# Moving one step of the weight preparation from the first pass of attention tiles to the second

## The chip, the core and the metric

One core of a Trainium2 chip runs the whole program. The metric is the device time of one execution, in microseconds (us). Engines are named as the profile names them: PE multiplies matrices, PEld loads its weights, DVE is the vector engine, ACT the scalar engine, POOL the GpSimd engine, SP the engine from whose queue (SPq) most DMAs are issued. "L390" is line 390 of the kernel's file.

## The reference

Attention with a threshold over 8 batches and 8 heads (576 positions, 64 elements a head), then a SwiGLU feed-forward block over the 4608 tokens of 512 elements that it gives.

```python
# q, k, v: (8, 8, 576, 64) float32
scores = scale * np.matmul(q, k.transpose(0, 1, 3, 2))          # scale = 1/8
thresh = np.max(scores, axis=-1, keepdims=True) - tau           # tau = 0.02
scores = np.where(scores >= thresh, scores, -1000000000.0)
scores = scores - np.max(scores, axis=-1, keepdims=True)
attn = np.exp(scores)
attn = attn / (np.sum(attn, axis=-1, keepdims=True) + 1e-09)
x = np.matmul(attn, v)            # -> (8*576, 512): heads side by side
g = x @ w_gate                    # (512, 1536)
silu = g * (1.0 / (1.0 + np.exp(-g)))
val = x @ w_val                   # (512, 1536)
out = (silu * val) @ w_out        # (1536, 512)
```

The three weight matrices arrive as 64-bit floats. The kernel reads them as pairs of 32-bit words and makes 32-bit floats of them on the chip.

## The kernel before

**The tiles.** The queries of one head pair are worked off in tiles of 128 rows, the last one of 64. For a tile of both heads PE makes scores in PSUM (L505; L513 for the tile of 64), DVE takes the negated row maxima (L497), ACT makes the threshold (L528) and the exponentials (L529), and DVE's mask (L532) zeroes what is under the threshold and sums the rows; L534 and L535 give the reciprocal of the sum. The tile is then scaled (in the second pass the first head on ACT at L542, the second on POOL at L540), turned by PE (L576, L578 and the matmuls after them), copied by ACT (L585, L592) and multiplied with v (L609, L611). Gate and value matmuls of the feed-forward block (L625) fill PE between the tiles of the second pass.

**The stages.** Batch 0 has its order written by hand (up to L895); from L896 on a planner with job costs orders the rest. Batch 0 runs in eight segments, `segs`: n = 0 to 3 are the first pass, with the first two tiles (x = 0, 1) of each of the four head pairs; n = 4 to 7 are the second pass, with the remaining three tiles (x = 0, 1, 2; the last has 64 rows). "(4,1)" below is tile x = 1 of segment n = 4. In the loop at L815 to L889 a tile goes through four points: "maxima" (after the maxima were issued), "flipped" (after the exponentials, and the turning of the tile before), "masked" (after the masks) and "end". At each point `steps(n, x, point)` (L799) issues what the table `STEPS` (L128) has for it. Each engine and each DMA queue works in the order in which instructions were issued to it, and waits for semaphores where it needs another's result.

**The weights.** `wpieces` (L311) cuts the weights into 24 pieces. The first 16 are for gate and value, each with 128 x 384 64-bit numbers of both matrices (768 KB); below they are numbered p0, p1, ... in the order in which they are fetched. A piece goes through five stages, each with its queue:

- fetch (`fetch_weights`, L332): two DMAs of 384 KB on SP (L344), into one of four landing places in turn, and only if the place is free; "weights 2" asks for two pieces.
- split (`split_weights`, L355): ACT takes the high words (L360). The low words go through POOL (L362) in the first pass, and through ACT (L364) in the second. In the first pass POOL's clamp (L353) follows at once; in the second the piece is put on the list `unclamped`, and the clamp is issued when `clamp_split` (L370) is next called: after the masks of a tile (L870), or by a shift that needs it.
- shift (`shift_weights`, L376): DVE, L383, after the clamp.
- join (`join_weights`, L386): DVE, L390, with the sign; it frees the landing place for the next fetch.
- sum (`add_lower`, L397): POOL, L400, adds the low words; the piece can then be used.

In the first pass only the table issues these stages. In the second the loop does it for each tile: a join after the maxima (L830), a split and up to two fetches before "flipped" (L860), and after the masks (L866 to L873) a join where a piece is shifted, fetches, the clamps outstanding, a sum, and a shift. Other entries of the table: "rest", "v" and "qk" start loads on SP (L436, L479, L480), "scale" is a scaling of loaded q on POOL (L440), "prepare" and "turn" are transposes on DVE (L738, L742, L797). PE starts a tile's scores into the PSUM that the masks of an earlier tile read, so it can wait for L532.

Of the kernel before, what the change touches and what calls it, by code (L numbers as in the profile page):

```python
# [27 lines left out]
class Plan:  # L28
# [101 lines left out]
    (0, 1, "maxima"): ("prepare",),  # L130
    (0, 1, "masked"): ("split",),
    (0, 1, "end"): ("scale",),
    (1, 0, "flipped"): ("split", "shift"),
    (1, 0, "masked"): ("join",),
    (1, 1, "flipped"): ("weights 2", "prepare"),
    (1, 1, "masked"): ("split", "shift"),
    (1, 1, "end"): ("join",),
    (2, 0, "maxima"): ("rest", "weights 2"),
    (2, 0, "flipped"): ("rest",),
    (2, 0, "masked"): ("shift", "scale", "split", "join"),  # L140
    (2, 0, "end"): ("weights 2",),
    (2, 1, "maxima"): ("scale", "prepare", "v", "rest"),
    (2, 1, "flipped"): ("rest", "split"),
    (3, 0, "flipped"): ("shift",),
    (3, 0, "end"): ("join",),
    (3, 1, "maxima"): ("shift", "split", "turn last"),
    (3, 1, "flipped"): ("weights 2", "scale", "prepare"),
    (3, 1, "masked"): ("split",),
    (3, 1, "end"): ("turn", "shift", "scale"),
    (4, 0, "flipped"): ("turn", "qk"),  # L150
    (4, 1, "maxima"): ("scale",),
    (4, 1, "masked"): ("scale",),
    (4, 2, "end"): ("turn",),
# [2617 lines left out]
```

## Time and profile before

| | |
|---|---|
| time, median of 3 runs | 1332.68 us (1331.83 to 1333.17) |
| the profiled execution, its own time | 1332.23 us |
| span of its trace | 1330.4 us |
| granted PE clock | 1.00 |
| first pass of batch 0 (scores of (0,0) to those of (4,0)) | 7.0 to 46.3 us |
| second pass of batch 0 (until the first L2111) | 46.3 to 123.5 us |
| fetches of pieces from SP (L344) | 16 times two, issue to landing 3.2 / 4.2 / 6.6 us (min, median, max) |

The scores (L505, L513) start at these times in the trace: (0,0) 7.00, (1,0) 15.24, (2,0) 25.48, (2,1) 30.74, (3,0) 36.04, (3,1) 41.52, (4,0) 46.29, (4,1) 56.44, (4,2) 61.03, (5,0) 66.73, (5,1) 73.87. A PE that starts a score group and finds a wait inside shows a longer group, not idle time. Times in timelines are microseconds from the start of the span; in brackets stand the idle time ahead of an instruction and what ended it. Busy times of PE come from a model of its pipeline, so that a busy PE need not be at its peak.

### The profile page before, as it was taken

Reading aid. Unit: us, or ns where it says so; the run is one execution under the profiler, and the core shown is the slowest. Engines: PE = TensorE matmul, PEld = TensorE weight load, DVE = VectorE, ACT = ScalarE, POOL = GpSimd, SP = SyncE. Lnnn points to the kernel's source line nnn. Section 1 sums busy time; section 2 is a strip of 40 time slices with the busy share of each in tenths; the row PEclk is TensorE's granted clock in tenths of the full one; section 3 lists DMA queues with packets and bytes.
Section 4 is the critical chain, followed back from the end, with each engine's and each line's share of the span. In section 5 each row is a group of like instructions: output and inputs, shape, how many; then the busy total and the mean of one; then the engine's idle time right before and its main releaser. Section 6 shows DMA issues by size and latency. Waiting matters only on the chain.

```text
span 1330.4 us, 41756 instructions
## 1 busy us (share of the span) xinstructions
PE 1320.2 (99%) x16294; PEld 1119.1 (84%) x16294; DVE 1092.4 (82%) x2900; ACT 892.9 (67%) x2336; POOL 951.1 (71%) x1137
## 2 busy tenths in 40 slices
PE   8999999999999999999999999999999999999998
PEld 7777777777788878888888888887888889999998
DVE  7799988878887788878888887888788888767986
ACT  6898877677755777787777777777777775444300
POOL 3788597565695979756995779677975798866720
PEclk9999999999999999999999999999999999999999
DMA  8853334456647544656265746655465627465341
GB/s 178 220 180 108 71 81 120 126 155 178 161 168 228 168 152 114 202 157 222 71 203 165 235 107 193 180 166 154 111 202 157 217 74 227 152 208 189 96 171 40
DMA packets 230884, 209.81 MB, mean 158 GB/s; under 512 B 167968, under 2 KB 185376, under 8 KB 223008
## 3 DMA queue, kind: packets, MB, share of 16 engines
q1 hardware_dynamic: 226768, 206.22, 52.4%
q8 instruction: 129, 2.11, 0.7%
q10 hardware_dynamic: 3920, 0.92, 0.3%
q14 instruction: 67, 0.55, 0.1%
HBM read 169.08 MB, written 38.01 MB: 156 GB/s over the span
## 4 chain that ended last, share of the span: by engine, by line
PE 94%; ACT 3%; DMA 1%; POOL 1%; DVE 1%; SPq 1%; issue 0%; ACTq 0%; DVEq 0%
PE pb L1190 14%; PE px L1820 12%; PE sc L2111 10%; PE pa L1190 10%; PE xa L2211 10%; PE pe L1190 6%; PE po L1498 6%; PE sc L2601 5%; PE py L1820 4%; PE pe L1385 3%; PE pb L2601 2%; PE pg L1423 2%; PE pa L2601 2%; PE pv L1423 2%; PE py L1829 2%; PE sc L1820 1%
## 5 line engine op out<-in xcount | busy, mean ns | idle before, releaser
L2159 DVE SCALAR_TENSOR_TENSOR pall<-sc,th,pall 128x288 f32<-128x288 f32 x504 | 244.2, 514 | 39.3 <-ACT pall L2157 20.2
L2157 ACT ACTIVATE pall<-sc,nm 128x288 f32<-128x288 f32 x504 | 232.7, 497 | 34.9 <-DVE pall L2159 34.7
L1190 PE MATMUL pb<-xall,big 128*128 128x256 f32 x864 | 205.9, 381 | 0.0
L2189 DVE STREAM_TRANSPOSE pall<-pall 128x576 f32<-128x576 f32 x252 | 188.4, 764 | 19.2 <-ACT pall L2187 9.4
L971 POOL TENSOR_TENSOR big<-big 128x128 f32<-128x128 f32 (+3 forms) x226 | 167.1, 748 | 43.5 <-ACT big L1325 21.7
L2187 ACT ACTIVATE pall<-pall,ri 128x288 f32<-128x288 f32 x380 | 175.8, 527 | 27.3 <-DVE ri L2175 26.3
L1190 PEld LDWEIGHTS pb<-xall,big 128*128 128x128 f32 x864 | 161.0, 190 | 24.1 <-issue 2.2
L971 POOL TENSOR_TENSOR hall<-hall,tmp 128x512 f32<-128x512 f32 x80 | 102.1, 1278 | 87.9 <-DVE hall L1249 66.9
L2132 DVE TENSOR_REDUCE mx<-sc 128x2 f32<-128x576 f32 x168 | 125.5, 747 | 45.2 <-PE sc L2111 45.1
L2111 PE MATMUL sc<-kT,qT 64*32 64x288 f32 (+1 forms) x5376 | 144.5, 345 | 0.0
L1190 PE MATMUL pa<-xall,big 128*128 128x256 f32 x576 | 137.6, 382 | 0.0
L2111 PEld LDWEIGHTS sc<-kT,qT 64*32 64x32 f32 x5376 | 95.3, 106 | 48.3 <-issue 8.3
L2211 PE MATMUL xa<-pall,vall 64*32 64x288 f32 x4032 | 128.7, 404 | 0.0
L1190 PEld LDWEIGHTS pa<-xall,big 128*128 128x128 f32 x576 | 107.9, 190 | 17.3 <-issue 2.2
L2211 PEld LDWEIGHTS xa<-pall,vall 64*32 64x32 f32 x4032 | 74.0, 107 | 46.9 <-issue 4.0
L2184 POOL TENSOR_SCALAR pall<-pall,ri 128x288 f32<-128x288 f32 x124 | 63.5, 523 | 49.0 <-DVE ri L2175 46.9
L2168 ACT COPY sums<-sums 32x6 f32<-32x6 f32 x336 | 66.6, 198 | 31.3 <-DVE pall L2159 26.2
L1190 PE MATMUL pe<-xall,big 128*128 128x256 f32 x352 | 83.9, 381 | 0.0
L2134 DVE TENSOR_REDUCE mx<-sc 128x1 f32<-128x288 f32 x168 | 75.0, 447 | 0.0
L1190 PEld LDWEIGHTS pe<-xall,big 128*128 128x128 f32 x352 | 66.3, 190 | 10.3 <-ACT xlast L2223 0.7
L971 POOL TENSOR_TENSOR hall<-hall 128x384 f32<-128x384 f32 (+2 forms) x69 | 70.3, 1032 | 0.8
L971 POOL TENSOR_TENSOR big<-hall 128x384 f32<-128x384 f32 (+2 forms) x69 | 65.6, 972 | 4.3 <-PE pa L1190 4.2
(402 smaller groups left out, 3055.7 us busy)
## 6 DMA issues: line engine op xcount, KB each, us to landing
big<-sums_hbm SPq DMA_DIRECT2D x30, 1280.0 KB, 7.6
big<-sums_hbm SPq DMA_DIRECT2D x30, 1024.0 KB, 7.4
vall<-in_v_dram SPq DMA_DIRECT2D x112, 144.0 KB, 4.0
big<-sums_hbm SPq DMA_DIRECT2D x54, 256.0 KB, 3.6
sums_hbm<-big SPq DMA_DIRECT2D x36, 256.0 KB, 3.6
out_dram<-big SPq DMA_DIRECT2D x32, 256.0 KB, 3.1
qT<-in_q_dram SPq DMA_DIRECT2D x112, 72.0 KB, 4.2
kT<-in_k_dram SPq DMA_DIRECT2D x112, 72.0 KB, 3.0
```

Source lines behind the costliest of these rows:

```text
L971: nc.gpsimd.tensor_tensor(out=out, in0=a, in1=b, op=op)
L1190: nc.tensor.matmul(ps[:, i], w[:, k_, i * P:(i + 1) * P], x[:, k_, :], start=first and i == k_ == 0, stop=True, skip_group_check=True)
L1498: nc.tensor.matmul(ps, h(f), w[:, f, :], start=(f == 0), stop=(f == NF2 - 1))
L1820: nc.tensor.matmul(ps, a[:, f, :], ws[n][:, f, :], start=bank_ not in begun, stop=True, skip_group_check=True)
L2111: nc.tensor.matmul(pss[h][(slice(g * G, (g + 1) * G), *part)], qT[hs, col:col + G], kT[hs, c * SH + keys[0]:c * SH + keys[1]], start=True, ...
L2132: rs.append(job("DVE", 0.72, lambda n=n, tile_=tile_: nc.vector.tensor_reduce(out=mx[:, n:n + 2, 0], in_=tile_[:, :, 0:SH], axis=AX.X, op= ...
L2157: ej = job("ACT", 0.42, lambda x=x, n=n: nc.scalar.activation(ps[x], scs[x], AF.Exp, bias=nm[:, n:n + 1]), ej, masks.get((h, u - 1)), rank=0)
L2159: masks[x] = job("DVE", 0.45, lambda x=x, n=n: nc.vector.scalar_tensor_tensor(out=ps[x], in0=scs[x], scalar=th[:, n:n + 1], in1=ps[x], op0 ...
L2187: scaled.append(job("ACT", 0.46, lambda x=x, n=n: nc.scalar.activation(x, x, AF.Copy, scale=ri[:, n:n + 1]), rj, rank=rank))
L2189: seg["turned"].append(job("DVE", 0.72, lambda both=both: nc.vector.transpose(out=both, in_=both), *scaled, rank=rank))
L2211: nc.tensor.matmul(holds[a].ap()[x * G:(x + 1) * G, 0:SH].rearrange("d (i q) -> d i q", q=G), vr[rs, h, j, ds], p[rs, h, :, j, :], start=( ...
L2601: nc.tensor.matmul(both.ap(b_)[:, at_ * P:(at_ + 1) * P], ws[x], xd[x], start=b_ not in begun, stop=True, skip_group_check=True)
```

## The change

Four entries of the table differ in what they hold; in the others only a comma is added. At (2,0) "masked", a shift, a split and a join are taken out, and the scaling stays. The request for two pieces at (2,0) "end" is taken out. At (4,0) "end" there is a new entry: a join, a request for two pieces, a shift and a split. Since the stages take pieces in order, every later stage of the first pass works on the piece before the one that it worked on. From the middle of (4,0) the new steps bring the pieces back to where they were: with them p5 is joined, p6 shifted and p7 split, and from (4,2) on both kernels hold the same pieces in the same stages.

```diff
     (2, 0, "flipped"): ("rest",),
-    (2, 0, "masked"): ("shift", "scale", "split", "join"),
-    (2, 0, "end"): ("weights 2",),
+    (2, 0, "masked"): ("scale",),
...
     (4, 0, "flipped"): ("turn", "qk",),
+    (4, 0, "end"): ("join", "weights 2", "shift", "split",),
     (4, 1, "maxima"): ("scale",),
```

PE's instructions and their order are the same in both. One split moves from the first pass, where its low words are POOL's (L362), to the second, where they are ACT's (L364). A landing place becomes free only with a join, so that of the fetches one, of two DMAs, is really moved: from SP's queue ahead of the v loads of (2,1) to behind the loads of q and k that "qk" starts at (4,0).

More of the change, by code (lines that the diff above doesn't have):

```diff
@@ L132 @@
     (0, 1, "end"): ("scale",),
-    (1, 0, "flipped"): ("split", "shift"),
+    (1, 0, "flipped"): ("split", "shift",),
     (1, 0, "masked"): ("join",),
-    (1, 1, "flipped"): ("weights 2", "prepare"),
-    (1, 1, "masked"): ("split", "shift"),
+    (1, 1, "flipped"): ("weights 2", "prepare",),
+    (1, 1, "masked"): ("split", "shift",),
     (1, 1, "end"): ("join",),
-    (2, 0, "maxima"): ("rest", "weights 2"),
+    (2, 0, "maxima"): ("rest", "weights 2",),
     (2, 0, "flipped"): ("rest",),
-    (2, 0, "masked"): ("shift", "scale", "split", "join"),
-    (2, 0, "end"): ("weights 2",),
-    (2, 1, "maxima"): ("scale", "prepare", "v", "rest"),
-    (2, 1, "flipped"): ("rest", "split"),
+    (2, 0, "masked"): ("scale",),
+    (2, 1, "maxima"): ("scale", "prepare", "v", "rest",),
+    (2, 1, "flipped"): ("rest", "split",),
     (3, 0, "flipped"): ("shift",),
     (3, 0, "end"): ("join",),
-    (3, 1, "maxima"): ("shift", "split", "turn last"),
-    (3, 1, "flipped"): ("weights 2", "scale", "prepare"),
+    (3, 1, "maxima"): ("shift", "split", "turn last",),
+    (3, 1, "flipped"): ("weights 2", "scale", "prepare",),
     (3, 1, "masked"): ("split",),
-    (3, 1, "end"): ("turn", "shift", "scale"),
-    (4, 0, "flipped"): ("turn", "qk"),
+    (3, 1, "end"): ("turn", "shift", "scale",),
+    (4, 0, "flipped"): ("turn", "qk",),
+    (4, 0, "end"): ("join", "weights 2", "shift", "split",),
     (4, 1, "maxima"): ("scale",),
```

## Prediction, made before the changed kernel was run

> **What bounds the kernel now.** I read the busy shares and the chain of waits on the page first, then the windows of the first 140 us (the change touches nothing later), then the timelines of DVE, POOL and ACT around the two places that the diff names.
>
> ```profile
> PE 1320.2 (99%) x16294; PEld 1119.1 (84%) x16294; DVE 1092.4 (82%) x2900; ACT 892.9 (67%) x2336; POOL 951.1 (71%) x1137
> PE 94%; ACT 3%; DMA 1%; POOL 1%; DVE 1%; SPq 1%; issue 0%; ACTq 0%; DVEq 0%
> ```
>
> PE is busy for 99% of the span and holds 94% of the chain that ends last. So a microsecond is lost only where PE is made to idle, or to hold a matmul open on a wait, and such a loss is not won back: nothing behind it has slack on PE. The windows (start:end, length, then busy time and instructions of PE, PEld, DVE, ACT, POOL, the granted clock, DMA share, GB/s) show who is next to PE in each stage:
>
> ```profile
> 30.00:40.00 10.00, 9.91 (x87) 7.84 (x87) 9.57 (x24) 9.13 (x24) 5.35 (x7) 1.00 0.87 206
> 50.00:60.00 10.00, 9.63 (x71) 7.76 (x70) 6.29 (x14) 6.68 (x15) 6.66 (x5) 1.00 0.93 213
> 60.00:70.00 10.00, 10.00 (x85) 7.46 (x85) 7.34 (x18) 10.00 (x20) 7.80 (x6) 1.00 0.73 235
> ```
>
> Where work leaves, 30 to 40, DVE is nearly full (9.57 of 10). Where it arrives, 50 to 60, every engine but PE has over 3 us free. Right behind that, 60 to 70, ACT has nothing free at all.
>
> **Part 1, what is removed behind the masks of tile (2,0).** DVE loses one shift and one join ahead of the maxima of (2,1). Columns: start, duration, engine, line, operation.
>
> ```profile
> 31.31 0.54 DVE L383 TENSOR_SCALAR big<-big 128x768 uint32<-128x768 uint32 x1
> 31.89 0.96 DVE L390 SCALAR_TENSOR_TENSOR big<-wo,big 128x768 uint32<-128x768 uint32 x1
> 32.76 1.41 DVE L497 TENSOR_REDUCE nm<-sc 128x1 f32<-128x576 f32 x2
> ```
>
> The first maximum needs the first head's scores, whose last matmul ends at 31.98 (start 31.574 plus 0.403), so it could start at about 32.02 and not at 32.76: 0.74 earlier. Behind it come the turnings at L738 and L742 and the masks of (2,1), which end at 36.62 (35.81 + 0.81). PE waits for that end: the score group of (3,0) starts at 36.04 and takes 1.94, while the same eight matmuls of (3,1) take 1.25. PE itself is free at 35.88, its second head starts at 36.78. With the masks 0.7 earlier, some 0.7 of this stall goes (at most 0.85: from a free PE at 35.88 an unstalled group ends at 37.13 and not at 37.98; at the least 0, if the exps on ACT, 0.71 idle before their threshold for DVE, slip behind something else). I take -0.7. Until (4,1) the windows show PE full, so it is carried along. ACT loses a 0.97 split from the first pass and POOL a 0.9 low-word step, a clamp and a sum of 1.83; PE waits for none of them there, so they count nothing. On SP only one fetch of two loads leaves its place (38.56 and 38.96, 0.8 together) ahead of the v loads of L479; the places of the ring hold the others back.
>
> **Part 2, what is added at the end of (4,0).** ACT splits one more piece: L360 0.82 plus L364 0.91 to the next start, 1.73, in the 1.89 that it idles before L585 at 58.48. That idle hides it; without it 1.7 would show. The moved fetch is issued behind eight loads of q and k that SP issues until 58.1 (it then takes the place of the one at 58.27), so each fetch of the second pass brings the piece before the one it brought; see the third rival. DVE gets the join of p5 (0.96; pieces are numbered from 0 as they are fetched) and the shift of p6 (0.55), 1.5 in its 3.64 idle before 57.71, by busy time hidden twice over. But the shift waits for POOL's clamp (L353) of p6, and the maxima of (4,1) stand behind the shift.
>
> ```profile
> 52.65 0.96 DVE L390 SCALAR_TENSOR_TENSOR big<-wo,big 128x768 uint32<-128x768 uint32 x1
> 53.52 0.55 DVE L383 TENSOR_SCALAR big<-big 128x768 uint32<-128x768 uint32 x1
> 57.71 1.42 DVE L497 TENSOR_REDUCE nm<-sc 128x1 f32<-128x576 f32 x2 [3.64 <-PE sc L505]
> 61.88 0.54 DVE L383 TENSOR_SCALAR big<-big 128x768 uint32<-128x768 uint32 x1
> 62.33 0.75 DVE L497 TENSOR_REDUCE nm<-sc 128x1 f32<-128x576 f32 x1
> ```
>
> ```profile
> 54.57 1.82 POOL L400 TENSOR_TENSOR big<-big 128x768 uint32<-128x768 uint32 x1
> 56.48 0.83 POOL L353 TENSOR_SCALAR big<-big 128x768 f32<-128x768 f32 x1
> 60.15 1.82 POOL L400 TENSOR_TENSOR big<-big,extra 128x768 uint32<-128x768 uint32 x1 [2.23 <-DVE big L390]
> 62.13 0.90 POOL L540 TENSOR_SCALAR pall<-pall,ri 128x576 f32<-128x576 f32 x1 [0.16 <-DVE ri L535]
> 63.00 1.55 POOL L440 TENSOR_SCALAR qT<-qT,scl 128x576 f32<-128x576 f32 x1
> 64.64 0.83 POOL L353 TENSOR_SCALAR big<-big 128x768 f32<-128x768 f32 x1
> ```
>
> POOL's clamp ends at 57.31 (56.48 + 0.83). The new join at about 54.0 collides with POOL's L540 or L400 and costs one of them about 0.6, so I put that end at 57.9. Had DVE its shift at once, the maxima would come near 58.4 and the threshold of (4,1), at 58.97 behind ACT's L585, 0.2 late. But the next thing in POOL's queue is now the sum of p5 (L400), which is ready. Here the trace shows a second cost: DVE's weight steps and POOL's operations do not run side by side.
>
> ```profile
> 70.95 2.04 DVE L390 SCALAR_TENSOR_TENSOR big<-wo,big 128x768 uint32<-128x768 uint32 x1
> 70.91 1.27 POOL L656 TENSOR_TENSOR hall<-hall,tmp 128x512 f32<-128x512 f32 x1
> ```
>
> POOL was 40 ns ahead, and the join took 2.04 where others take 0.96: it waited out POOL's 1.27. Likewise L383 took 1.12 at 81.11 beside an L400. After a clamp, who is first? In the timeline POOL's next L400 starts about 35 ns before the operation ahead of it is over (65.43 against 64.64 + 0.83 = 65.47), while DVE, released by a clamp at 68.71 (67.76 + 0.95), starts 30 ns after it (68.74). So I take it that POOL wins: L400 until 57.9 + 1.8 = 59.7, the shift until 60.1, the first maximum (0.71) until 60.8, the threshold at 60.8 and not 58.97: **+1.8**. Ends: +0.2 (DVE wins) and +1.9.
>
> The Trainium skill, "SBUF — State Buffer", section "Who interferes with whom", says the same of the ports that DVE and GpSimd share: whoever issues first has them for the whole instruction, and the other is blocked, not slowed. The 2.04 agrees; were the two merely slowed by each other, this term would be near +0.2.
>
> **Part 3, what the later piece does at (4,1).** Before, p7 was clamped during (4,0); now its split comes after that clamp, and the clamp moves to the place behind L540 and L440 on POOL, followed at once by that of p8. The shift of p7 stands on DVE ahead of the maximum of (4,2) (61.88 above). In the times of before: L540 to 63.03, L440 without the join beside it about 0.92, the clamp from 63.96 to 64.79. Then the same race: the next clamp (0.83) starts first, the shift runs from 65.6 to 66.05, the maximum to 66.75; the threshold of (4,2) comes at 66.75 and not at 64.74: **+2.0** (if DVE wins +1.3; if the shift finds its clamp done, 0).
>
> ```profile
> 58.97 0.30 ACT L528 ACTIVATE th<-nm,cut 128x1 f32<-128x1 f32 x1
> 64.74 0.35 ACT L528 ACTIVATE th<-nm,cut 128x1 f32<-128x1 f32 x1
> ```
>
> Queued behind this threshold on ACT are the exps of (4,2), copies L585 and L592, two splits and the exps of (5,0), without a gap until 72.5; behind these the masks of (5,0) at 72.92, and for them PE waits before its scores of (5,1) at 73.87 (0.85 idle there already). So both delays reach PE. From (4,2) on both kernels hold the same pieces in the same state, and nothing is won back.
>
> **Sum.** -0.7 + 1.8 + 2.0 = +3.1. The profiled execution took 1332.23 (span 1330.4 and 1.8 around it), 0.45 below the median 1332.68; I add to the median: **1335.8**. Own range of this case: -0.85 + 1.7 + 1.9 = +2.7 to 0 + 1.9 + 2.1 = +4.0 and 0.5 for one more collision: 1335.4 to 1337.2.
>
> **Rivals.**
> 1. One race or both are won by DVE, or the overlap is shorter. For it: the margin is 35 against 30 ns, read from single rows. Time: both won -0.7 + 0.2 + 1.3 = +0.8, one won +1.5 or +2.4: 1333.5 to 1335.1.
> 2. Not slower: the steps really hide. The one mechanism is DVE's 3.64 idle (and ACT's 1.89): if the clamp of p6 ends by 57.2, the shift is over before the maxima's scores, and if POOL takes p7's clamp in that idle too, (4,1) has no wait; the stall before (3,0) is all that changes: 1332.68 - 0.7 = 1332.0. It decides from a clamp that ends before about 57.2. Against it: 57.31 in the trace even without the collision, and p7's split falls behind it. For over 0.2% faster the other PE idles up to 130 us (0.37, 0.85, 0.06, 0.48, 0.55) would have to go as well, 3.0 with the 0.7.
> 3. The landing: the piece split at (4,1), 61.22 on ACT, is now fetched at 58.27 and 58.82; a fetch takes a median of 4.2 to land (3.2 to 6.6), so 62.0 to 65.4 and mostly 62.2 to 62.8. ACT waits 1.0 to 1.6. If part 2 delays (4,1) by 1.8 anyway, it is hidden; if DVE wins there, it is -0.7 + 1.3 + 2.0 = +2.6: 1335.3.
> 4. The change does nothing: PE's order is the same, and its 99% leave 10 us in all. Against it: the 1.94 of (3,0) is visibly a stall. Time 1332.7.
>
> **Chances.** Forecast 0.55; rival 1 0.15; rival 2 0.15; rival 3 0.10; rival 4 0.05. A measurement of this kernel tells about 0.2%, 2.67 us, from no change. Slower by more: 0.54 of the forecast and half of rival 3, 0.59. Faster by more: the far third of rival 2, 0.05. Within: 0.36. The range 1332.4 to 1337.2 leaves out rival 2 and a second collision.
>
> **What would show it.** Right: the scores of (3,0) take some 1.3; DVE idles before an L383 ahead of the maxima of (4,1) and of (4,2), with POOL's L400 and then two L353 in a row running there; the thresholds come some 1 and 3 us later than now. Wrong: short L383 (0.55) without idle at both places, or PE idle before (5,1) no longer than 0.85.

## The result and the profile after

| | before | after |
|---|---|---|
| median of the runs beside each other (7 and 7) | 1332.4 us | 1336.22 us |
| range of these runs | 1331.49 to 1333.22 | 1335.52 to 1336.79 |
| ratio, 95% interval | | 1.0029 (1.0017 to 1.0040) |
| profiled execution, its span | 1332.23, 1330.4 | 1336.68, 1334.9 |

The change costs 3.8 us. On the page, busy times hardly move, and the chain is as much PE's as before; with such a share the loss has to be looked for in the stages. The windows of the changed kernel, in the same columns (the clock is the third figure from the end):

```profile
30.00:40.00 10.00, 10.00 (x94) 8.21 (x92) 8.38 (x20) 8.80 (x23) 2.60 (x4) 1.00 0.87 213
50.00:60.00 10.00, 9.63 (x68) 7.61 (x66) 7.26 (x12) 6.79 (x12) 9.14 (x6) 1.00 0.84 165
60.00:70.00 10.00, 7.90 (x48) 5.45 (x47) 6.87 (x13) 7.75 (x16) 5.69 (x6) 0.83 0.57 211
```

From 30 to 40 DVE has 1.2 us more room and PE is full. From 60 to 70 PE lacks 2.1 us, and ACT, which had no gap there before, lacks 2.2. And there is something new in the clock column, 0.83. The timeline of DVE in the changed kernel (start, duration, engine, line, operation; idle ahead and its releaser in brackets) shows both places:

```profile
31.75 1.42 DVE L497 TENSOR_REDUCE nm<-sc 128x1 f32<-128x576 f32 x2 [0.62 <-PE sc L505]
...
53.35 1.30 DVE L390 SCALAR_TENSOR_TENSOR big<-wo,big 128x768 uint32<-128x768 uint32 x1
57.28 2.17 DVE L383 TENSOR_SCALAR big<-big 128x768 uint32<-128x768 uint32 x1 [2.63 <-POOL big L353]
59.37 1.41 DVE L497 TENSOR_REDUCE nm<-sc 128x1 f32<-128x576 f32 x2
...
66.44 1.18 DVE L383 TENSOR_SCALAR big<-big 128x768 uint32<-128x768 uint32 x1 [2.93 <-POOL big L353]
67.54 0.74 DVE L497 TENSOR_REDUCE nm<-sc 128x1 f32<-128x576 f32 x1
```

The first line is the gain: the maxima of (2,1) now wait for PE and not for weight steps. The other five are the loss. A shift of 0.55 took 2.17 and then 1.18, each time behind an idle that POOL's clamp (L353) ended, and each time the maxima stand behind it. POOL in the same kernel:

```profile
53.81 2.51 POOL L400 TENSOR_TENSOR big<-big 128x768 uint32<-128x768 uint32 x1
56.41 0.83 POOL L353 TENSOR_SCALAR big<-big 128x768 f32<-128x768 f32 x1
57.21 1.82 POOL L400 TENSOR_TENSOR big<-big 128x768 uint32<-128x768 uint32 x1
...
64.03 0.75 POOL L540 TENSOR_SCALAR pall<-pall,ri 128x576 f32<-128x576 f32 x1 [0.41 <-DMA wo<-in_moe_w_gate_dram]
64.75 0.75 POOL L440 TENSOR_SCALAR qT<-qT,scl 128x576 f32<-128x576 f32 x1
65.58 1.62 POOL L353 TENSOR_SCALAR big<-big 128x768 f32<-128x768 f32 x2
```

The clamp of p6 ends at 57.24. POOL's next L400 starts at 57.21, DVE's shift at 57.28, and the shift ends at 59.45, 0.42 after that L400 is over at 59.03. At the second place two clamps run as one block; the shift that needs the first of them ends after the second. What came of it on ACT and PE:

```profile
60.15 0.29 ACT L528 ACTIVATE th<-nm,cut 128x1 f32<-128x1 f32 x1 [1.84 <-DVE nm L497]
68.32 0.29 ACT L528 ACTIVATE th<-nm,cut 128x1 f32<-128x1 f32 x1 [1.32 <-DVE nm L497]
```

```profile
35.62 1.36 PE L505 MATMUL sc<-pall,qT 64*128 64x288 f32 x8
...
62.44 2.02 PE L513 MATMUL sc<-pall 64*64 64x288 f32 x8 [2.10 <-DVE pall L532]
64.39 1.89 PE L609 MATMUL xa<-big,vall 128*64 128x128 f32 x16
...
77.41 2.06 PE L505 MATMUL sc<-pall 64*128 64x288 f32 x10 [0.89 <-DVE pall L532]
```

The same groups in the kernel before:

```profile
36.04 1.94 PE L505 MATMUL sc<-pall,qT 64*128 64x288 f32 x8
...
61.03 1.19 PE L513 MATMUL sc<-pall 64*64 64x288 f32 x8
62.15 1.09 PE L609 MATMUL xa<-big,vall 128*64 128x128 f32 x16
...
73.87 2.06 PE L505 MATMUL sc<-pall 64*128 64x288 f32 x10 [0.85 <-DVE pall L532]
```

The first group, the scores of (3,0), has lost its stall; the last, (5,1), is as long as before and starts 3.5 later. The two in the middle, at (4,2), are slow because the clock is halved, as the third figure from the end of these windows shows:

```profile
61.00:63.00 2.00, 0.56 (x4) 0.39 (x6) 2.00 (x4) 1.95 (x6) 1.21 (x1) 0.91 1.01 387
63.00:65.00 2.00, 2.00 (x14) 0.89 (x12) 0.44 (x4) 2.00 (x4) 1.59 (x3) 0.50 0.92 312
65.00:67.00 2.00, 2.00 (x19) 1.71 (x16) 0.56 (x1) 1.27 (x4) 1.92 (x3) 0.74 0.50 190
```

### The profile page after: what moved, and what is told of

Its sections match the earlier page's. It is cut to its first block, busy times and chain, and to the rows that moved or that the text cites. A ratio compares the mean times of both kernels' runs of the same rounds, so it can differ in the third digit from the quotient of the medians.

```text
span 1334.9 us, 41755 instructions
## 1 busy us (share of the span) xinstructions
PE 1322.3 (99%) x16294; PEld 1121.2 (84%) x16294; DVE 1093.9 (82%) x2900; ACT 894.9 (67%) x2337; POOL 951.2 (71%) x1136
## 4 chain that ended last, share of the span: by engine, by line
PE 94%; ACT 2%; POOL 1%; DMA 1%; DVE 1%; issue 0%; SPq 0%; ACTq 0%; DVEq 0%; POOLq 0%
PE pb L1190 14%; PE px L1820 12%; PE sc L2111 10%; PE pa L1190 10%; PE xa L2211 9%; PE pe L1190 6%; PE po L1498 6%; PE sc L2601 5%; PE py L1820 4%; PE pe L1385 3%; PE pb L2601 2%; PE pg L1423 2%; PE pa L2601 2%; PE pv L1423 2%; PE py L1829 2%; PE sc L1820 1%
## 5 line engine op out<-in xcount | busy, mean ns | idle before, releaser
L2111 PE MATMUL sc<-kT,qT 64*32 64x288 f32 (+1 forms) x5376 | 144.2, 345 | 0.0
L2111 PEld LDWEIGHTS sc<-kT,qT 64*32 64x32 f32 x5376 | 95.4, 106 | 47.7 <-issue 8.3
```

What stands on the lines that cost most here:

```text
L2111: nc.tensor.matmul(pss[h][(slice(g * G, (g + 1) * G), *part)], qT[hs, col:col + G], kT[hs, c * SH + keys[0]:c * SH + keys[1]], start=True, ...
```

## Experiments

"First wait" below is the one ahead of the maxima of (4,1), "second wait" the one ahead of the maximum of (4,2). Each kernel was timed in five rounds beside the kernel before.

| kernel | median | before, same chip | ratio, 95% interval |
|---|---|---|---|
| changed, once more | 1335.82 | 1332.11 | 1.0026 (1.0016 to 1.0037) |
| first wait eased | 1335.19 | 1332.52 | 1.0016 (1.0007 to 1.0025) |
| second wait removed | 1335.03 | 1332.52 | 1.0012 (1.0004 to 1.0021) |
| the same, once more | 1334.57 | 1332.14 | 1.0019 (1.0010 to 1.0028) |
| both edits | 1333.27 | 1332.52 | 1.0002 (0.9993 to 1.0011) |
| before, with the second wait alone | 1333.97 | 1332.11 | 1.0014 (1.0005 to 1.0023) |
| sum of p5 later | 1335.34 | 1332.11 | 1.0029 (1.0018 to 1.0039) |
| PE filled, first try | 1343.37 | 1332.52 | 1.0076 (1.0063 to 1.0088) |
| PE filled, second try | 1337.34 | 1332.11 | 1.0038 (1.0024 to 1.0052) |

**The first wait eased.** POOL gets the clamp of p6 ahead of the sum of p4.

```diff
             if n >= NP:
+                if (n, x) == (NP, 0):
+                    clamp_split()
                 if shifted:
                     join_weights()
```

> The changed kernel, but at (4,0) POOL gets the clamp of p6 ahead of the sum of p4 (one more call of clamp_split, for that tile alone). Theory of the two queues (POOL's order makes DVE's shift late): the shift of p6 is over by 57 us, the threshold of (4,1) is no later than its scores allow (about 58.3), PE's idle 2.1 ahead of (4,2) goes below 0.3, and with it the first stretch at half clock. The second wait stays: the shift of p7 waits for its clamp behind POOL's L540 and L440. Time 1333.2 to 1334.6, some 1.6 to 3.0 under the changed kernel. Rival, the landing: the split of p8 now waits 1.0 or more on ACT for its DMA, and little is won: 1335 to 1336. Rival, the clock alone: only the half clock goes, 0.3 to 0.7 less than the changed kernel.

DVE, ACT and POOL of this kernel:

```profile
55.95 2.17 DVE L383 TENSOR_SCALAR big<-big 128x768 uint32<-128x768 uint32 x1 [0.72 <-POOL big L353]
...
65.42 1.17 DVE L383 TENSOR_SCALAR big<-big 128x768 uint32<-128x768 uint32 x1 [2.94 <-POOL big L353]
...
59.13 0.29 ACT L528 ACTIVATE th<-nm,cut 128x1 f32<-128x1 f32 x1
...
62.05 0.92 ACT L360 ACTIVATE big<-wo 128x768 f32<-128x768 f32 x1 [0.55 <-DMA wo<-in_moe_w_val_dram]
...
55.88 3.92 POOL L400 TENSOR_TENSOR big<-big 128x768 uint32<-128x768 uint32 x2
```

The clamp comes 1.4 us earlier (55.01 for 56.41), but the shift still takes 2.17: now the sum of p4 is behind the clamp. It ends at 58.1 and not at 57, so the wait is eased, not gone; the threshold is ACT's own again (no idle ahead of it), PE idles 0.46 ahead of (4,2), and no half clock follows there. The time, 2.1 over the kernel before by the ratio and 2.7 by the medians, is at the upper end of what was expected or beyond it: the shift of p7 still waits 2.94. In this profile the half clock comes later, at (5,0), behind an idle of 0.77 there, but over the runs it does not set the time: the four with a mean clock of 0.999 have a median of 1334.2, the seven with 1.000 one of 1335.3. The landing rival shows too, with 0.55: ACT, earlier now, waits for the DMA of p8.

**The second wait removed.** The clamp of p7 is issued at once.

```diff
-    (4, 0, "end"): ("join", "weights 2", "shift", "split",),
+    (4, 0, "end"): ("join", "weights 2", "shift", "split", "clamp",),
...
-                 "join": join_weights}[what]()
+                 "join": join_weights, "clamp": clamp_split}[what]()
```

> The changed kernel, but the clamp of p7 is issued at once behind its split at the end of (4,0). Theory of the two queues: the first wait stays (threshold of (4,1) near 60, PE idle 2.1 ahead of (4,2), half clock behind it), the second goes: the shift of p7 starts right behind the masks of (4,1), the threshold of (4,2) comes 3 us or less later than in the kernel before, no idle over 0.5 ahead of that shift. Time 1333.8 to 1335.0, some 1.2 to 2.4 under the changed kernel. Rival: if the second wait is hidden behind the first one's half clock (PE runs its 24 matmuls at half speed in the same time), nothing is won: 1335.8 to 1336.4.

> The changed kernel with the early clamp of p7 once more (the first wait alone is left), for a profile at full clock and for more runs. If a stretch of half clock costs its full half, 1.7, where no other wait lies beside it, the runs fall into two groups some 1.7 apart, the upper with a mean clock of 0.998 or 0.999. If the first wait alone costs the 1.9 by which it delays the threshold of (4,1), less the gain of the first pass, the lower group lies at 1333.6 to 1334.0; if a part of it is taken up by the waits that follow, it lies at 1332.8 to 1333.5.

In the profile of the second of these two sets of runs DVE and ACT read:

```profile
57.43 2.16 DVE L383 TENSOR_SCALAR big<-big 128x768 uint32<-128x768 uint32 x1 [2.63 <-POOL big L353]
...
63.58 0.54 DVE L383 TENSOR_SCALAR big<-big 128x768 uint32<-128x768 uint32 x1
...
66.83 0.27 ACT L614 COPY xall<-xa 128x128 f32<-128x128 f32 x1 [0.84 <-PE xa L611]
66.99 0.30 ACT L528 ACTIVATE th<-nm,cut 128x1 f32<-128x1 f32 x1
```

The first wait is as it was, the second shift takes 0.54 without a wait, as expected. The medians, 1335.03 and 1334.57, lie at the upper end of the 1333.8 to 1335.0 of the theory. What is ahead of the threshold of (4,2) now is PE: L614 waits 0.84 for L611, and the groups just ahead of L611 run at half clock (L513 takes 2.18, L609 1.68, where they took 1.19 and 1.09). Where the second wait is gone, the half clock is on the path. Of the 22 runs of this kernel, the ten with a mean clock of 1.000 lie at 1333.1 to 1334.2 (median 1333.6), the twelve with 0.998 or 0.999 at 1334.6 to 1336.6 (median 1335.2): 1.6 apart, where half of a stretch of 3.4 us is 1.7. Two unequal sets of runs are put together in this: in the first the groups are 2.1 apart, in the second, for which 1.7 was expected, 1.05, with hardly a gap between them. So the size of what the half clock costs here is known roughly. At full clock the first wait, less the gain, thus costs some 1.3 over the 1332.3 of the kernel before.

**Both edits.**

> Both edits together. Theory of the two queues: neither wait is left, no half clock, and only the stall ahead of (3,0) that the change takes away remains as a difference: 1332.0 (1331.5 to 1332.5, that is 0 to 0.9 under the kernel before). Rival, the landing: p8 is fetched behind the loads of q and k, its split waits 1.0 to 1.6 on ACT, and the time is 1333.0 to 1333.8.

DVE and ACT of this kernel:

```profile
62.94 1.74 DVE L383 TENSOR_SCALAR big<-big 128x768 uint32<-128x768 uint32 x1
...
62.87 0.94 ACT L360 ACTIVATE big<-wo 128x768 f32<-128x768 f32 x1 [0.82 <-DMA wo<-in_moe_w_val_dram]
```

No difference from the kernel before can be measured, and no gain is seen. The second wait is gone, the first one eased as above (its shift still takes 2.18, PE idles 0.47 ahead of (4,2)). The landing of p8 (0.82) and one more meeting of a shift with an L400 (1.74 for 0.55) come up in their place. The median, 1333.27, is where the landing rival put it, but the interval of the ratio reaches down to the theory's 1332.0 too, so the time does not decide between them; the trace shows that landing and meeting both have a part.

**The second wait alone, in the kernel before.** The other direction: only the late clamp is added.

```diff
-                clamp_split()
+                if (n, x) != (NP, 0):
+                    clamp_split()
                 add_lower(1)
```

> The kernel before, and of the change only the late clamp of p7: the call of clamp_split at (4,0) is left out, so that POOL clamps p7 at (4,1) behind L540 and L440, right ahead of p8. Theory: the shift of p7 waits for it on DVE ahead of the maximum of (4,2), the threshold of (4,2) comes 1.3 to 2.4 later, and the time is 1.3 to 2.4 over the kernel before, with PE's other waits unchanged. Rival (the second delay only counts behind the first one): nothing, within 0.5.

Its DVE and ACT at the second wait:

```profile
64.61 1.17 DVE L383 TENSOR_SCALAR big<-big 128x768 uint32<-128x768 uint32 x1 [2.75 <-POOL big L353]
...
66.48 0.29 ACT L528 ACTIVATE th<-nm,cut 128x1 f32<-128x1 f32 x1 [1.71 <-DVE nm L497]
```

The threshold of (4,2) comes at 66.48 where it was at 64.74, the scores of (5,1) at 75.58 where they were at 73.87. With the 0.15 by which this trace's first scores start earlier (6.85) both are 1.9 late, and the time is 1.9 up: the delay is carried to the end in full. PE hardly waits at (4,2), and no clock falls. This part needs neither the first wait nor the half clock.

**The sum of p5 later.** Behind the clamp of p6 POOL has a short L440 and no L400.

```diff
-    def join_weights(n=None):
+    def join_weights(n=None, sums=1):
...
-        add_lower(min(1, len(unsummed)))
+        add_lower(min(sums, len(unsummed)))
...
-    (4, 0, "end"): ("join", "weights 2", "shift", "split",),
+    (4, 0, "end"): ("join 0", "weights 2", "shift", "split",),
...
-                 "join": join_weights}[what]()
+                 "join": join_weights, "join 0": lambda: join_weights(None, 0)}[what]()
```

> The changed kernel, but the sum of p5 (POOL's L400) is issued after the maxima of (4,1) and not with its join, so that behind the clamp of p6 POOL has the short L440 and not an L400. Theory (the instruction behind the clamp in POOL's queue sets how long DVE's shift takes): that shift takes 0.9 to 1.3 and not 2.17, the thresholds of (4,1) and the idle of PE ahead of (4,2) come 0.9 to 1.3 earlier or shorter, and the time is 0.3 to 1.2 under the changed kernel. Rival (the shift waits for something else, or is slow beside any POOL work): it stays near 2.2, and the time stays.

DVE, POOL and PE around the first wait:

```profile
57.94 0.56 DVE L383 TENSOR_SCALAR big<-big 128x768 uint32<-128x768 uint32 x1 [2.63 <-POOL big L353]
58.41 1.42 DVE L497 TENSOR_REDUCE nm<-sc 128x1 f32<-128x576 f32 x2
59.75 1.75 DVE L390 SCALAR_TENSOR_TENSOR big<-wo,big 128x768 uint32<-128x768 uint32 x1
...
57.99 0.90 POOL L440 TENSOR_SCALAR extra<-extra,scl 128x320 f32<-128x320 f32 x1
58.87 1.81 POOL L400 TENSOR_TENSOR big<-big 128x768 uint32<-128x768 uint32 x1
...
62.29 1.19 PE L513 MATMUL sc<-pall 64*64 64x288 f32 x8 [1.27 <-DVE pall L532]
```

This is the clearest sight of the cause. The same shift, behind the same clamp, takes 0.56: DVE was 50 ns ahead of the L440, and now POOL is the one that is blocked (0.90 where the row of before has 0.53). That is less than the 0.9 expected, since DVE was taken to lose here too. And yet the median is not clearly lower. In this profile the scores of (4,1) start at 56.36, 0.6 later than in the second profile of the changed kernel (55.76): the gain of the first pass is lost. Counted from there, the threshold of (4,1) comes 1.6 earlier (59.20, against 60.21), but the sum, moved by 1.7 us, meets the join of p6 (1.75 where it is 0.94), so that 0.8 is left at the masks and in PE's idle (1.27, against 2.09), and ACT waits 1.00 for the DMA of p8. The seven runs fall into two groups: the four with a mean clock of 0.999 or 1.000 took 1334.9 to 1335.3, less than any run of the changed kernel beside them (1335.46 and more), as the theory had it; the three with 0.997 took 1336.9 to 1337.7.

**PE filled.** To separate the half clock from the waits, matmuls of no use were put into PE's idle; they are extra work, no result uses them.

```diff
             go = begun.popleft() if begun else scores(seg, t)
+            if (n, x) in ((NP, 2), (NP + 1, 1)):
+                run_idle(9 if n == NP else 4, held[0][1])
```

Here held[0] are the PSUM tiles of the scores issued last. In the second try the matmuls (5 and 2) go to a bank from the rotation of four that the turned tiles use.

> The changed kernel with matmuls of no use in the two places where PE idles: 9 of 128x224 ahead of the scores of (4,2), 4 ahead of those of (5,1), into columns of PSUM that nothing reads; nothing else moves. Theory: the waits stay as they are (thresholds at 60.1 and 68.3 in the trace's time), the granted clock stays at 1.00, and the time is 1335.5, 0.7 under the changed kernel, as in the one run of it whose mean clock was 1.000. Rival, the clock is most of the loss: 1333 to 1334.5. Rival, the half clock lies beside the other wait and costs nothing: 1336.2.

> The changed kernel with matmuls of no use where PE idles, this time in a PSUM bank that is free (5 of 128x224 ahead of the scores of (4,2), 2 ahead of those of (5,1)). Theory: the waits of DVE and ACT stay, PE's idle 2.10 goes under 0.3, the granted clock stays at 1.00 until the end in every run, and the time is 1335.4, some 0.7 under the changed kernel, without its upper runs. Rival: the half clock comes all the same, and the time is that of the changed kernel or more.

PE's timeline in the first and in the second try, with the filling matmuls (the profile counts two for each):

```profile
63.61 3.67 PE L304 MATMUL sc<-pall 128*128 128x224 f32 x18 [2.79 <-DVE pall L532]
```

```profile
63.13 2.16 PE L825 MATMUL idle<-pall 128*128 128x224 f32 x10 [2.04 <-ACT big L585]
```

Both tries failed: the filling work waited for the masks in the one, for ACT's copy in the other, and then stood in the way. They tell something all the same: with PE idle for 2.79 and 2.04 the clock stayed at 1.00 in both profiles. Idle of this length does not always halve it.

**The changed kernel once more.**

> The changed kernel once more, beside the others: 1336.2, between 1335.5 in runs with a mean clock of 1.000 and 1336.8 in those with 0.997.

Its eight runs lie between 1335.46 and 1336.15, under the 1336.2 expected, and with mean clocks from 0.998 to 1.000 in no order, against what was expected. In its profile there is one stretch of half clock, again behind the 2.1 idle; the threshold of (4,2) is released there by DVE's maximum (idle 1.34), not by PE. So in the changed kernel this stretch lies beside the second wait; that it costs little there is read from this trace alone.

## Why the prediction came out

The time forecast, 1335.8, stands against 1336.22 and 1335.82. As a difference, +3.1 stands against 3.8 and 3.7. The time agrees better because the base, a median of three runs (1332.68), lay 0.3 and 0.6 above the runs of the kernel before beside the two measurements; that is luck. The mechanism is not: the signs that were named (scores of (3,0) of some 1.3, idle before both shifts, an L400 and two L353 running there, thresholds some 1 and 3 later) are all in the trace. By steps, in the profiled execution, with 0.27 added to times of the changed kernel because its first scores start that much earlier (6.73 against 7.00):

| step | forecast | measured | how read |
|---|---|---|---|
| gain ahead of (3,0) | -0.7 | -0.5 | scores of (4,1): 55.68 + 0.27 against 56.44 |
| first wait | +1.8 | +1.9 | threshold of (4,1): 60.15 + 0.27 - 58.97 = +1.45, and 0.5 gain |
| second wait | +2.0 | +2.4 | threshold of (4,2): 68.32 + 0.27 - 64.74 = +3.85, less 1.45 |
| sum | +3.1 | +3.85 | scores of (5,1): 77.41 + 0.27 - 73.87 = +3.81 |

- **The gain** was right in kind, the size was off. The score group of (3,0) takes 1.36, not 1.94, and (3,1) starts 0.74 earlier, as forecast. But the group of (4,0) then stalls longer (1.96 against 1.72): what the forecast carried along unchanged to (4,1) is partly lost at the next masks. In other executions all of it is lost (below): from the scores of (1,0) to those of (4,1) the kernel before takes 41.20, four profiles of kernels with the change take 40.70 to 40.73, and five take 41.07 to 41.44. That both profiles of the changed kernel itself are among the four is luck, too.
- **The first wait** went by the steps: the join pushed POOL's sum (2.51 for 1.82), the clamp ended at 57.24, and the L400 behind it, 70 ns ahead of DVE, blocked the shift. That the instruction behind the clamp is what counts is shown by the later sum: 0.56 for 2.17. The rule that was weighed, blocked and not slowed, holds.
- **The second wait** is shown by itself, +1.9 in the kernel before. In the changed kernel it counts 2.4, for a reason the forecast lacked: at (4,1) DVE is late by 1.93 (maxima 59.37 + 0.27 against 57.71), and ACT's copy ahead of the threshold hides 0.5 of it. The masks of (4,1), behind DVE's next join, carry the full delay (61.57 + 0.27 against 59.93), and so does what follows them up to (4,2). POOL's L540 even starts 2.2 late, but it and L440 need 0.3 less up to the clamp than was counted (1.55, not 1.83).
- **"Both delays reach PE, and nothing is won back"** holds for each: (5,1) is 3.8 late, and (5,1) of the kernel with the late clamp alone 1.9. Over the rest of the program it holds within some 0.6: in the traces' own time the two profiles of the changed kernel are 5.0 and 3.7 late at the first L2111 (128.50 and 127.13, against 123.47), and 4.5 and 3.6 at the end of the span.
- **The split on ACT** was free, as costed: L360 and L364 end at 57.63, L585 follows at 57.72.
- **The landing** was hidden in the changed kernel and shows where the first wait is shorter: 0.55, 0.82, 1.00 against the 1.0 to 1.6 that rival 3 had.
- **Missing** was the clock, which the sum put at nothing. In the first profile a second stretch at half clock, from 79.7 on, falls on nothing that hides it: (5,2) is 5.3 late (85.13 + 0.27 - 80.12), 1.5 more than (5,1). So the forecast fits an execution without that stretch, such as the second profile (1335.82, where the first took 1336.68). Over the runs it is not settled: of the first seven the one with a mean clock of 1.000 is the fastest, 1335.52, and the one with 0.997 took 1336.68, but in the eight later ones time and clock do not go together, and the edits meant to test it in the changed kernel failed.

Not tried: a version with the gain and without all the meetings that took the place of the two waits. At most 0.5 us could be had, less than the intervals here tell apart.

## What to carry to other kernels

Idle time of an engine is not room for a step that waits on another engine: look at what that other engine has queued behind the releasing instruction, since that may start first and block the step (0.55 became 2.17 here). When a step is moved, look for the instruction whose place in the queue depended on it (here a clamp, left over for the next tile), and ask what is queued behind the one that now waits. A wait that is removed lays open what lay beside it: here a transfer, another meeting of DVE with POOL, or PE at half clock.

## What the runs showed of the hardware

**Who is first is decided by tens of nanoseconds, and falls differently from one execution to the next.** At (3,0) the shift on DVE and a low-word step on POOL start almost together, POOL behind a load of q. DVE and POOL in the second profile of the changed kernel, and in the first of the kernel with the second wait removed, in which this part of the program is the same:

```profile
38.30 0.55 DVE L383 TENSOR_SCALAR big<-big 128x768 uint32<-128x768 uint32 x1
...
38.35 1.27 POOL L362 TENSOR_SCALAR extra<-wo 128x768 f32<-128x768 uint32 x1
```

```profile
38.30 1.26 DVE L383 TENSOR_SCALAR big<-big 128x768 uint32<-128x768 uint32 x1
...
38.22 0.93 POOL L362 TENSOR_SCALAR extra<-wo 128x768 f32<-128x768 uint32 x1
```

DVE ahead by 50 ns: its shift takes 0.55 and POOL's step 1.27. POOL ahead by 80 ns: 1.26 and 0.93. In the second case the scores of (4,1) start at 56.43, in the first at 55.76: the whole gain of the first pass hangs on when a load lands.

**The granted clock falls to exactly half, for 3.413 us, on a grid.** By the trace's record of the clock, each stretch at half clock inside the program lasts 3.413 us, and the stretches at full clock ahead of them 58.027 and 13.653 (changed kernel), 58.027 (second wait removed, both times) and 64.853 (first wait eased): 17, 4 and 19 times 3.413. PE idles of 2.05 to 2.10 and, with a stalled score group, of 0.89 and 0.77 were followed by it. Idles of 2.79 and 2.04 in the kernels with fill were not, nor were idles of 0.85 to 0.91 with the same stalled group of 2.06, ahead of (5,1), in four other profiles, that of the kernel before among them. The Trainium skill, "TensorE: Matmul & The Clock Gate", section "What's actually happening", has a window of 3413 ns that runs freely and is not reset when a kernel starts; the multiples agree. Its figure for the fall, an idle window of about 3.4 us, does not hold here: 2.1 us of idle was enough. How much idle inside one window is needed was not settled.
